# Attention and two feed-forward layers: the products with w_in by seven block products instead of eight

## The chip, the cores and the metric

The kernel runs on one core of one Trainium2 chip. The metric is the device time of one execution in microseconds (us). TensorE (PE) multiplies matrices, its weight loads are listed as PEld; VectorE (DVE), ScalarE (ACT) and GpSimd (POOL) work on elements; SyncE (SP) issues the DMAs. A "column" is one column of the moving operand of a matmul, 128 deep.

## The reference

```python
scores = scale * np.matmul(q, k.transpose(0, 1, 3, 2))          # 4 batches, 8 heads, 576 tokens, 64 wide
cum = np.cumsum(np.log(np.clip(f, 0.0001, 1.0)), axis=-1)
scores = np.where(causal, -1000000000.0, scores + cum[:, :, :, None] - cum[:, :, None, :])
attn = softmax(scores)                                           # row maximum taken off, sum + 1e-9
x = (attn @ v).transpose(0, 2, 1, 3).reshape(2304, 512)
h = x @ moe_w_in;  x = (h - np.tanh(h)) @ moe_w_out              # w_in 512 x 2048, w_out 2048 x 512
h = x @ moe2_w_in; return (h * (1 / (1 + np.exp(-h)))) @ moe2_w_out
```

The weights arrive in double precision, the other inputs in single.

## The kernel before

**Attention** takes about the first 179 us. It goes over 16 pairs of heads, nine tiles each (144 tiles, then a tail), and puts its result, features on partitions, into `x` of 4 x 2304 columns. The list `ahead` places work of the feed-forward part between its tiles, counted from the last tile: weight loads and decoding, the split of the first inputs, and the first twelve pieces of products with w_in (`hidden`).

**High and low parts.** A single-precision operand is kept as two tiles of the type TensorE multiplies: the high part is a cast on ScalarE, the low part the rest, a subtraction on VectorE. A product is three matmuls, high x high, high x low and low x high, into one sum in PSUM. The doubles are decoded into such pairs by seven steps on ScalarE and VectorE (`wstages`).

**Feed-forward.** The 2048 hidden features are 16 chunks of 128, in three sets a layer (`SETS`); the tokens are five groups (four of 512, one of 256). Loops: layer, set, group, chunk. A step multiplies the group's four input tiles with the chunk's w_in (`hidden`, 12 matmuls into one PSUM bank), two steps later its gate with the chunk's w_out (`project`, 12 matmuls into accumulators of PSUM). Between, `gate` computes h - tanh(h) in layer 0 (tanh on ScalarE, line 268, the difference on VectorE, line 269) or silu in layer 1 (line 271), the cast of the high part (line 272) and the low part (line 275). At a set's end the accumulators are copied or added to the total, a tile `y` for layer 0; layer 1's goes back into `x`, and its last set through `ob` (three buffers, line 320) to the output, one DMA of 256 KB for each 128 tokens. Inputs are split once for each set and group (`xsplit`).

**Order.** It is written out by hand: every engine executes its instructions in the order of the program. `front(n)` issues step n's w_in products, the next group's split, step n - 1's gate, and a share of the decoding for the next set; `project` follows.

Of the kernel before, what the change touches and what calls it, by code (L numbers as in the profile page):

```python
# [39 lines left out]
def forgetting_attention_two_ffn(  # L40
# [81 lines left out]
    z = x.rearrange("p k t -> p (k t)").rearrange("p (m d) -> p m d", d=DM)  # L122
    ys = []

    wtiles, raws = {}, {}  # L130

    chunks = [(l, c) for l in range(2) for c in range(NFC)]

    def wload(k, ms=(0, 1)):
        if k >= len(chunks):
            return
        l, c = chunks[k]
        for m in ms:
            r = rawp.tile([P, DM, 2], U32, tag="raw", name=f"raw{l}_{c}_{m}")
            nc.sync.dma_start(out=r.rearrange("p n w -> p (n w)"), in_=(w_in, w_out)[m][l][c])  # L140
            raws[k, m] = r

    def wstages(k):

        l, c = chunks[k]
        slot = k % NSLOT
        tag = {m: f"{l}_{c}_{m}" for m in range(2)}
        a, b, w = {}, {}, {}

        def scale(m):  # L150
            high = rd(raws[k, m][:, :, 1])
            nc.scalar.activation(high, high, AF.Prelu, scale=2.0 ** -112, alpha=-(2.0 ** 32))

        def shift(m):
            a[m] = wtmp.tile([P, DM], U32, tag="wa", name=f"wa{tag[m]}")
            nc.vector.tensor_scalar(a[m], raws[k, m][:, :, 1], 3, None, ALU.logical_shift_left)

        def split(m):
            hi, lo = w[m] = [
                wpool[slot].tile([P, DM], F32R, tag=f"w{s}{slot}_{m}", name=f"w{s}{tag[m]}") for s in "hl"  # L160
            ]
            nc.scalar.copy(hi, rd(a[m]))

        def exponent(m):
            b[m] = wtmp.tile([P, DM], F32, tag="wb", name=f"wb{tag[m]}")
            nc.vector.tensor_scalar(b[m].bitcast(U32), a[m], 0xFF800000, None, ALU.bitwise_and)

        def low(m):
            nc.vector.scalar_tensor_tensor(
                b[m], raws.pop((k, m))[:, :, 0], 2.0 ** -52, b[m], ALU.mult, ALU.mult  # L170
            )

        def rest(m):
            hi, lo = w[m]
            nc.vector.tensor_tensor(lo, rd(a[m]), rd(hi), ALU.subtract)

        def join(m):
            hi, lo = w[m]
            nc.vector.tensor_tensor(lo, rd(lo), b[m], ALU.add)
            wtiles[l, c, m] = (hi, lo)  # L180

        return [(fn, m) for fn in (scale, shift, exponent, low, split, rest, join) for m in range(2)]
# [560 lines left out]
```

## Time and profile before

| | |
|---|---|
| median of 3 runs | 968.22 us (968.2 to 968.56) |
| the profiled execution | 968.29 us |
| its span, first to last instruction | 966.5 us |
| busy TensorE / VectorE / ScalarE / POOL | 958.9 / 564.0 / 456.7 / 161.0 us |
| granted TensorE clock, mean | 0.999 |
| DMA | 56.67 MB, of it 64 weight tiles of 512 KB |

An engine's busy time is the union of its instructions. Matmuls overlap in the records, so the mean length of one is longer than the step from one start to the next. Idle time is put down to the engine whose work ended it.

### The profile page before, as it was taken

What the parts mean: (1) busy time and instruction counts of PE and PEld (TensorE: products, weight loads), DVE (VectorE), ACT (ScalarE), POOL (GpSimd) and SP (SyncE); (2) the same over time, 40 slices, a digit from 0 to 9 for tenths busy, and PEclk for the clock granted to TensorE, in tenths of its full rate; (3) what the DMA queues carried; (4) which work ended last, traced back from release to release, by engine and by line L of the source; (5) the groups of instructions that cost most, each with busy time, mean ns of one, the idle gap of its engine ahead of it and who ended that gap; (6) DMA issues with size and microseconds to landing.
All of it is one profiled execution on the core that took longest, in us unless ns stands there. A gap on an engine that the chain in (4) does not pass through costs nothing.

```text
span 966.5 us, 13852 instructions
## 1 busy us (share of the span) xinstructions
PE 958.9 (99%) x5208; PEld 791.4 (82%) x5208; DVE 564.0 (58%) x1243; ACT 456.7 (47%) x979; POOL 161.0 (17%) x244
## 2 busy tenths in 40 slices
PE   8999999999999999999999999999999999999998
PEld 6777777789888889888888888888888888888887
DVE  7788888767764657555767743344344555523323
ACT  6788888545444334333434443344344443433322
POOL 8999999100000000000000000000000000000000
PEclk9999999999999999999999999999999999999999
DMA  5343342221210111110122101010111110001111
GB/s 165 140 137 125 125 161 81 107 87 45 88 44 1 44 45 44 44 44 0 44 87 82 50 1 44 22 66 0 44 44 44 44 44 1 1 1 43 44 44 66
DMA packets 21698, 56.67 MB, mean 59 GB/s; under 512 B 6848, under 2 KB 6848, under 8 KB 21600
## 3 DMA queue, kind: packets, MB, share of 16 engines
q1 hardware_dynamic: 21624, 55.77, 16.8%
q8 instruction: 41, 0.67, 0.3%
q14 instruction: 25, 0.20, 0.1%
q10 hardware_dynamic: 8, 0.02, 0.0%
HBM read 49.35 MB, written 5.31 MB: 57 GB/s over the span
## 4 chain that ended last, share of the span: by engine, by line
PE 98%; DVE 1%; POOL 0%; DMA 0%; issue 0%; ACT 0%; POOLq 0%
PE h L254 41%; PE a L312 41%; PE t L494 5%; PE s L447 5%; PE out_t L550 4%; PE s L439 2%; PE out L550 0%; PE out_t L578 0%; DMA de<-x 0%; DVE x L113 0%; DVE x L111 0%; DVE p L460 0%; DVE de L571 0%; DVE x L117 0%; POOL p L482 0%
## 5 line engine op out<-in xcount | busy, mean ns | idle before, releaser
L254 PE MATMUL h<-xh,wh 128*128 128x512 f32 (+1 forms) x640 | 236.0, 369 | 0.0
L254 PE MATMUL h<-xl,wh 128*128 128x512 f32 (+1 forms) x640 | 235.6, 368 | 0.0
L254 PE MATMUL h<-xh,wl 128*128 128x512 f32 (+1 forms) x640 | 235.4, 368 | 0.0
L275 DVE TENSOR_TENSOR gl<-g,gh 128x512 fp32r<-128x512 f32 (+1 forms) x160 | 101.9, 637 | 103.4 <-ACT gh L272 101.6
L254 PEld LDWEIGHTS h<-xh,wh 128*128 128x128 f32 x640 | 120.7, 189 | 20.7
L254 PEld LDWEIGHTS h<-xl,wh 128*128 128x128 f32 x640 | 120.6, 188 | 20.4
L254 PEld LDWEIGHTS h<-xh,wl 128*128 128x128 f32 x640 | 120.6, 188 | 20.1
L272 ACT CAST gh<-g 128x512 fp32r<-128x512 f32 (+1 forms) x160 | 92.6, 579 | 92.8 <-DVE g L269 90.2
L312 PE MATMUL a<-gl,wh 128*128 128x512 f32 (+1 forms) x320 | 117.8, 368 | 0.0
L312 PE MATMUL a<-gh,wh 128*128 128x512 f32 (+1 forms) x320 | 117.7, 368 | 0.0
L312 PE MATMUL a<-gh,wl 128*128 128x512 f32 (+1 forms) x320 | 117.7, 368 | 0.0
L312 PE MATMUL a<-wh,gh 128*128 128x512 f32 x288 | 112.2, 390 | 0.0
L312 PE MATMUL a<-wl,gh 128*128 128x512 f32 x288 | 112.2, 390 | 0.0
L312 PE MATMUL a<-wh,gl 128*128 128x512 f32 x288 | 112.0, 389 | 0.0
L271 ACT ACTIVATE g<-h 128x512 f32<-128x512 f32 (+1 forms) x80 | 44.3, 554 | 115.3 <-PE h L254 95.2
L242 DVE TENSOR_TENSOR xl<-y,xh 128x512 fp32r<-128x512 f32 (+1 forms) x60 | 37.4, 638 | 96.4 <-ACT xh L240 96.4
L240 ACT CAST xh<-y 128x512 fp32r<-128x512 f32 (+1 forms) x60 | 34.2, 580 | 105.4 <-PE h L254 103.7
L468 ACT ACTIVATE p<-p,mn 128x128 f32<-128x128 f32 (+3 forms) x128 | 71.2, 558 | 15.1 <-DVE mn L460 12.7
L482 POOL TENSOR_SCALAR p<-p,sm 128x128 f32<-128x128 f32 (+3 forms) x128 | 71.4, 577 | 8.6 <-DVE sm L479 7.9
L242 DVE TENSOR_TENSOR xl<-x,xh 128x512 fp32r<-128x512 f32 (+1 forms) x56 | 34.5, 634 | 63.9 <-ACT xh L240 63.9
L460 DVE CUSTOM_DVE_ANT_0 p<-s,mask 128x128 f32<-128x128 f32 (+3 forms) x128 | 59.5, 480 | 20.1 <-PE s L447 20.1
L312 PEld LDWEIGHTS a<-gh,wh 128*128 128x128 f32 x320 | 60.3, 189 | 10.1
(89 smaller groups left out, 1368.7 us busy)
## 6 DMA issues: line engine op xcount, KB each, us to landing
raw<-w_in SPq DMA_DIRECT2D x32, 512.0 KB
raw<-w_out SPq DMA_DIRECT2D x32, 512.0 KB
kqraw<-kq SPq DMA_DIRECT2D x16, 608.0 KB
vraw<-v SPq DMA_DIRECT2D x16, 320.0 KB
out<-ob SPq DMA_DIRECT2D x18, 256.0 KB
lq<-kqs SPq DMA_DIRECT2D x32, 32.0 KB
dec<-x SPq DMA_DIRECT2D x1, 576.0 KB
de<-dec SPq DMA_DIRECT2D x28, 17.0 KB
```

Of the source, the lines that this page charges most:

```text
L242: eng.tensor_tensor(lo[:, :n], src[:, k, t0:t0 + n], rd(hi[:, :n]), ALU.subtract)
L254: nc.tensor.matmul(hp[:, :n], w[:, k * P:k * P + P], m[:, :n], start=(k == 0 and r == 0), stop=(k == NKT - 1 and r == 2),)
L271: nc.scalar.activation(g[:, :n], hp[:, :n], AF.Silu)
L272: nc.scalar.copy(gh[:, :n], g[:, :n])
L275: nc.vector.tensor_tensor(gl[:, :n], g[:, :n], rd(gh[:, :n]), ALU.subtract)
L312: nc.tensor.matmul(dst, w, m, start=(first and r == 0), stop=(last and r == 2))
L447: nc.tensor.matmul(s[:, h, c:c + n], a[half(h), q], b[half(h), 0:n], start=r == 0, stop=r == 3,)
L460: nc.vector.tensor_tensor_reduce(out=pt.rearrange("p (g c) -> p g c", g=2) if i == 4 else pt, in0=src, in1=m, op0=ALU.add, op1=ALU.min, sc ...
L468: nc.scalar.activation(pt, pt, AF.Exp, bias=mn, scale=-1.0, accum_out=sums[:, n // 3 % 5, n % 3, 0:1],)
L482: nc.gpsimd.tensor_scalar(pt, pt, sm[:, j:j + 1], 1.0, ALU.mult, ALU.mult)
L494: nc.tensor.transpose(t[:, k], pt[:, c * P:c * P + P], ident)
L550: nc.tensor.matmul(dst, vraw[p][:, h, D * c:D * c + D], ptfs[p % 2][:, h, 448 * c + a:448 * c + q1], start=c == 0, stop=c == last,)
```

## The change

The products with w_in are done in Strassen's way (with Winograd's sums). A block is 768 tokens; its input is a 2 x 2 of blocks (two halves of the 512 features, 256 each, by two halves of the tokens, 384 each), and the weights of two chunks are a 2 x 2 too (two chunks by two halves of the features). Seven products replace eight. Their operands are sums and differences of blocks: four sums of weights on VectorE for each pair of chunks, four differences of inputs for each block of tokens (`xtemp`), and the products are combined by seven additions on VectorE (`add`), which also take them off PSUM; product 1 is copied by ScalarE.

Loops: layer, set (now four sets of two pairs), block (three), pair. One pair for one block is a **slot**, 48 in all; a layer, set and block is a unit of two slots. A slot is fifteen pieces, seven products (six matmuls of 384 columns each) and eight pieces G of products with w_out ("halves") that belong to gates of the slots before: `P1 G P6 G P2 G G P7 G P5 G P4 G P3 G`. In layer 0 a half is six matmuls of 384 columns; in layer 1 six or three of 512. Slot 0 has no halves, slot 1 has two; after the last slot 14 halves follow.

The seven operands of a block, each split into high and low, are made in the first set of a layer (`xmake`), and written to DRAM, 786 KB each; in the other sets each is loaded again (`xload`) after its last product of the unit before. Every operand has one buffer. The weights' decoding works on two chunks at once, with low and high joined before the sums, and is spread over the pieces by a table (`fills`). The attention tail has no products with w_in any more; it makes the first block's operands and decodes pair 1. Accumulators have two buffers of two banks, products four of one bank. The first set's totals are copied by ScalarE, all others are added by VectorE. There is no `y`: layer 0's result goes into `x` again. `ob` has one buffer, for two output tiles.

```diff
-HL = 2
-NEARLY, MID, LATE = 2, 3, 6
-SETS = ((5, 6, 5), (6, 5, 5))
+NB, TB, TH = 3, 768, 384
+KA = {1: 1, 2: 2, 3: 6, 4: 0, 5: 3, 6: 4, 7: 5}
...
-    rawp = ctx.enter_context(tc.tile_pool(name="rawp", bufs=4))
-    wtmp = ctx.enter_context(tc.tile_pool(name="wtmp", bufs=3))
+    rawp = ctx.enter_context(tc.tile_pool(name="rawp", bufs=2))
+    wtmp = ctx.enter_context(tc.tile_pool(name="wtmp", bufs=1))
...
+            to, p, op, r = ((4, 0, ALU.add, 1), (6, 2, ALU.subtract, 0),
+                            (5, 4, ALU.subtract, 2), (7, 3, ALU.subtract, 5))[part]
+            nc.vector.tensor_tensor(s[:, to], s[:, p], s[:, r], op)
...
+    for s in range(2 * NSET):
+        e, o, k = 2 * s + 2, 2 * s + 3, 6 * s
+        first = s == 0
+        plan = {
+            1 + first: jobs(e, 0, [("scale",)], PRE),
+            2 + first: jobs(e, 0, SUMS, HILO) + jobs(e, 1, [("scale",)]),
+            3 + first: jobs(e, 1, PRE, LAST),
+            4 + first: jobs(o, 0, [("scale",)], PRE, SUMS),
+            6: jobs(o, 1, PRE),
+        }
+        plan[5] = plan.get(5, []) + jobs(o, 0, HILO) + jobs(o, 1, [("scale",)])
+        for d, js in plan.items():
+            fills.setdefault(k + d, []).extend(js)
+        late.add(k + 7)
+        fills.setdefault(k + 7, []).extend(jobs(o, 1, LAST))
+    fills[0] = jobs(1, 0, HILO) + jobs(1, 1, [("scale",)], PRE)
+    fills[1] = jobs(1, 1, LAST)
...
+        to, p, m = ((t1, b12, b11), (t2, b22, t1), (t1, b22, b12), (t2, b21, t2))[k - 1]
+        nc.vector.tensor_tensor(to, p, m, ALU.subtract)
...
+        nc.scalar.copy(t[:, 0], frm)
+        (eng or nc.vector).tensor_tensor(t[:, 1], frm, rd(t[:, 0]), ALU.subtract)
+        d = xd[l, b, i] = dram.tile([P, 4 * TH], F32, name=f"xd{l}_{b}_{i}")
+        nc.sync.dma_start(out=d, in_=rd(t).rearrange("p r k t -> p (r k t)"))
+
+    def xload(u, i):
+        l, s, b = units[u]
+        t = xtile(u, i)
+        nc.sync.dma_start(out=rd(t).rearrange("p r k t -> p (r k t)"), in_=xd[l, b, i])
...
+        if s == 0:
+            xat(2 * u - 2, 5, xtemp, l, b, 1)
+            xat(2 * u - 2, 6, xtemp, l, b, 2)
+            for p, i in ((2, 1), (4, 6), (6, 2)):
+                xat(2 * u - 1, p, xmake, u, i)
+            xat(2 * u - 1, 7, xtemp, l, b, 4)
+            xat(2 * u - 1, 11, xmake, u, 5)
+            xat(2 * u - 1, 12, xtemp, l, b, 3)
+            xat(2 * u - 1, 13, xmake, u, 7)
+            xat(2 * u, 0, xmake, u, 4)
+            xat(2 * u, 2, xmake, u, 3)
+        else:
+            for i, p in PIECE.items():
+                xat(2 * u - 1, p, xload, u, i)
...
+        if s == 0:
+            nc.scalar.copy(total, acc)
+        elif l == 0 or s + 1 < NSET:
+            nc.vector.tensor_tensor(total, acc, total, ALU.add)
+        else:
+            ob = wtmp.tile([P, 2, DM], F32, tag="wb", name=f"ob{u}_{h}_{g}")
...
+    def bend(u, j, h):
+        l = units[u][0]
+        t = pools["tp"].tile([P, 2, TH], F32, tag=f"t{h}", name=f"t{u}_{j}_{h}")
+        nc.scalar.activation(t, hs[h], AF.Silu if l else AF.Tanh)
         if l == 0:
+            nc.vector.tensor_tensor(t, hs[h], t, ALU.subtract)
...
+                i = int(what[1])
+                dst = product(u, j, i)
+                if i == 1:
+                    nc.scalar.copy(half_tile(u, j, 0)[:, 1], dst)
+                    rest()
+                elif i == 6:
+                    add(half_tile(u, j, 1)[:, 0], dst, hs[0][:, 1])
+                elif i == 2:
+                    add(hs[0][:, 1], dst, hs[0][:, 1])
+                elif i == 7:
+                    add(hs[0][:, 0], dst, hs[1][:, 0])
+                elif i == 5:
+                    add(hs[1][:, 1], dst, hs[1][:, 0])
+                    add(hs[1][:, 0], dst, hs[0][:, 0])
+                elif i == 4:
+                    add(hs[0][:, 0], dst, hs[0][:, 0])
+                    bend(u, j, 0)
+                else:
+                    add(hs[1][:, 1], dst, hs[1][:, 1])
+                    high(u, j, 0)
+                    low(u, j, 0)
+                    bend(u, j, 1)
+                    left.extend([(high, (u, j, 1)), (low, (u, j, 1))])
+            for fn, a in xplan.get((sl, p), []):
+                fn(*a)
+            for job in todo[slice(*share.get(p, (0, 0)))]:
+                fill(job)
...
-            for i in range(3):
-                for k in range(NKT):
-                    at(4 * i + k, hidden, i, [k])
...
+            for n, i in ((-11, 1), (-8, 2)):
+                at(n, xmake, 0, i, nc.gpsimd)
+            for n, k in ((-1, 1), (0, 2), (2, 4), (4, 3)):
+                at(n, xtemp, 0, 0, k)
+            for n, i in ((1, 6), (3, 5), (5, 7), (6, 4), (7, 3)):
+                at(n, xmake, 0, i)
+            for k, job in enumerate(jobs(1, 0, [("scale",)], PRE, SUMS)):
+                at(8 + k, fill, job)
```

The fills go in equal shares behind ten pieces of a slot (1 to 7, 11, 12 and 14, counted from 0). `PRE` is shift, exponent, low and join; `HILO` the high and low parts of the seven w_in operands in two portions each; `LAST` those of w_out.

## Rows read from the trace of the kernel before

**Rows 1.** Page, busy us and share; then forty slices, tenths; GB/s a slice.

```profile
PE 958.9 (99%) x5208; PEld 791.4 (82%) x5208; DVE 564.0 (58%) x1243; ACT 456.7 (47%) x979; POOL 161.0 (17%) x244
...
PE   8999999999999999999999999999999999999998
...
PEclk9999999999999999999999999999999999999999
...
GB/s 165 140 137 125 125 161 81 107 87 45 88 44 1 44 45 44 44 44 0 44 87 82 50 1 44 22 66 0 44 44 44 44 44 1 1 1 43 44 44 66
```

**Rows 2.** Page, chain that ended last, shares of the span by line.

```profile
PE h L254 41%; PE a L312 41%; PE t L494 5%; PE s L447 5%; PE out_t L550 4%; PE s L439 2%; PE out L550 0%; PE out_t L578 0%; DMA de<-x 0%; DVE x L113 0%; DVE x L111 0%; DVE p L460 0%; DVE de L571 0%; DVE x L117 0%; POOL p L482 0%
```

**Rows 3.** Timeline of TensorE around 223 us: start us, us, engine, operation.

```profile
221.00 0.39 PE L312 MATMUL a<-gh,wh 128*128 128x512 f32 x1
...
223.72 0.28 PE L254 MATMUL h<-xh,wh 128*128 128x256 f32 x1
...
225.15 0.40 PE L312 MATMUL a<-gh,wh 128*128 128x512 f32 x1
```

**Rows 4.** Groups by form, TensorE: count | busy us, mean ns | idle us.

```profile
L254 PE MATMUL h<-xh,wh 128*128 128x512 f32 x512 | 199.9, 390 | 0.0
...
L312 PE MATMUL a<-wh,gh 128*128 128x512 f32 x288 | 112.2, 390 | 0.0
...
L312 PE MATMUL a<-gh,wh 128*128 128x512 f32 x256 | 99.7, 389 | 0.0
...
L254 PE MATMUL h<-xh,wl 128*128 128x256 f32 x128 | 36.2, 283 | 0.0
...
L312 PE MATMUL a<-gh,wh 128*128 128x256 f32 x64 | 18.1, 282 | 0.0
```

**Rows 5.** Timeline of VectorE, 184 to 190 us; in brackets idle us and releaser.

```profile
184.52 1.28 DVE L169 SCALAR_TENSOR_TENSOR wb<-raw,wb 128x512 f32<-128x512 uint32 x2
185.72 1.29 DVE L175 TENSOR_TENSOR wl<-wa,wh 128x512 fp32r<-128x512 f32 x2
...
189.50 0.69 DVE L275 TENSOR_TENSOR gl<-g,gh 128x512 fp32r<-128x512 f32 x1 [0.69 <-ACT gh L272]
```

**Rows 6.** Groups by form, VectorE and ScalarE.

```profile
L275 DVE TENSOR_TENSOR gl<-g,gh 128x512 fp32r<-128x512 f32 x128 | 88.4, 690 | 91.5 <-ACT gh L272 89.9
L272 ACT CAST gh<-g 128x512 fp32r<-128x512 f32 x128 | 79.6, 622 | 74.9 <-DVE g L269 72.8
...
L166 DVE TENSOR_SCALAR wb<-wa 128x512 uint32<-128x512 uint32 x64 | 26.6, 442 | 0.0
...
L275 DVE TENSOR_TENSOR gl<-g,gh 128x256 fp32r<-128x256 f32 x32 | 13.5, 421 | 11.8 <-ACT gh L272 11.7
L272 ACT CAST gh<-g 128x256 fp32r<-128x256 f32 x32 | 13.0, 407 | 17.9 <-DVE g L269 17.4
```

**Rows 7.** Timelines of POOL, TensorE and VectorE, end of attention.

```profile
171.21 0.75 POOL L482 TENSOR_SCALAR pt<-pt,sm 128x576 f32<-128x576 f32 x1
...
171.33 0.48 PE L254 MATMUL h<-xh,wh 128*128 128x512 f32 x1
...
176.16 0.40 PE L254 MATMUL h<-xh,wl 128*128 128x512 f32 x1
...
176.65 2.76 PE L550 MATMUL out_t<-ptf,vraw 128*64 128x512 f32 x20
...
177.41 0.28 DVE L539 COPY ptf<-t 128x128 f32<-128x128 f32 x1
```

**Rows 8.** Timeline of VectorE, last output adds.

```profile
949.54 2.06 DVE L321 TENSOR_TENSOR ob<-a,x 128x512 f32<-128x512 f32 x3 [3.36 <-PE a L312]
952.41 0.69 DVE L321 TENSOR_TENSOR ob<-a,x 128x512 f32<-128x512 f32 x1 [0.81 <-DMA out<-ob]
```

**Rows 9.** Chain of waits in order of time, its last piece: start us, us.

```profile
962.77 0.69 DVE ob L321
```

**Rows 10.** DMA rate, 300 to 400 us, in 40 slices of 2.5 us.

```profile
GB/s 7 0 0 0 0 0 0 0 0 0 0 285 141 0 0 0 0 3 3 67 143 0 0 182 34 0 0 0 33 338 56 0 0 0 0 0 28 270 121 0
```

More of the change, by code (lines that the diff above doesn't have):

```diff
@@ L121, in forgetting_attention_two_ffn @@
     x = xpool.tile([P, NKT, NT], F32, name="x")
[L122 to L182, printed above, removed]
@@ L219, in forgetting_attention_two_ffn @@
-    pools, xs, hps, gts, accs = {}, {}, {}, {}, {}
-    def ends(i):
-        si, c = steps[i][1], steps[i][5]
-        c0 = sum(SETS[steps[i][0]][:si])
-        return c == c0, c == c0 + SETS[steps[i][0]][si] - 1
+    units = [(l, s, b) for l in range(2) for s in range(NSET) for b in range(NB)]
+    NSL = 2 * len(units)
+    pools = {}
     def open_pools(bank=None, **bufs):
@@ new lines, in forgetting_attention_two_ffn, with wload, wdo @@
+    raws, wtiles, wjobs = {}, {}, {}
+    ODD_FIRST = (1, 0)
+    def wload(q, m, parts=(0, 1)):
+        if q >= 2 * NPR:
+            return
+        l, c = divmod(2 * q, NFC)
+        if (q, m) not in raws:
+            raws[q, m] = rawp.tile([P, 2, DM, 2], U32, tag="raw", name=f"raw{q}_{m}")
+        for i in parts:
+            to = raws[q, m][:, i].rearrange("p n w -> p (n w)")
+            nc.sync.dma_start(out=to, in_=(w_in, w_out)[m][l][c + ODD_FIRST[i]])
+    def wdo(q, *names):
+        for name in names:
+            wjob(q, *name)
@@ new lines, in forgetting_attention_two_ffn, with jobs @@
+    PRE = [(w,) for w in ("shift", "exponent", "low", "join")]
+    SUMS = [("sum", k) for k in range(4)]
+    HILO = [("hi", 0), ("hi", 1), ("lo", 0), ("lo", 1)]
+    LAST = [("hi",), ("lo",)]
+    def jobs(q, m, *lists):
+        return [(q, m) + j for js in lists for j in js] if q < 2 * NPR else []
+    fills, late = {}, set()
+    for s in range(2 * NSET):
[13 more added lines that the diff above has]
+        fills.setdefault(k + 7, []).extend(jobs(o, 1, LAST))
@@ new lines, in product @@
+    def product(u, j, i):
+        q = 2 * (u // NB) + j
+        wih, wil = (w[:, KA[i]] for w in wtiles[q, 0])
+        xh, xl = xo[u, i][:, 0], xo[u, i][:, 1]
+        dst = pools["ps_h"].tile([P, 512], F32, tag="h", name=f"h{u}_{j}_{i}")[:, 0:TH]
+        for k in range(2):
+            ks = slice(k * P, k * P + P)
+            for r, (w, m) in enumerate(((wih, xh), (wih, xl), (wil, xh))):
+                nc.tensor.matmul(dst, w[:, ks], m[:, k], start=k == 0 and r == 0, stop=k == 1 and r == 2)
+        return dst
```

300 lines of the change are left out of this document (169 added, 131 removed).

## The prediction

> **What bounds the kernel now.** I read the busy line and the slices first. TensorE's queue is never empty: 99% busy, nine tenths in every slice but the first and last, at a granted clock of nine tenths or more, while VectorE has 58% and ScalarE 47% over the span [rows 1]. A busy TensorE need not be a limiting one, so the chain of waits comes next: its TensorE lines add up to 98%, 41% of it the products with w_in (line 254) and 41% those with w_out (line 312) [rows 2]. Third, the step between starts, because a matmul's listed length (390 ns at 512 columns) overlaps its neighbours. Twelve matmuls of 512 columns take 223.72 - 221.00 = 2.72 us, 226.7 ns each; twelve of 256 take 225.15 - 223.72 = 1.43 us, 119.2 ns each [rows 3]. Both are the columns at 2.4 GHz (213.3 and 106.7 ns) plus some 13 ns. The weight load of each matmul is hidden, or the shorter ones could not step at 119 ns. So 384 columns, half-way between, get 173.0 ns.
>
> **1. TensorE's work.** Before, the feed-forward part holds, by its groups: with w_in 3 x 512 at 512 columns and 3 x 128 at 256; with w_out, layer 0, 3 x 256 at 512 and 3 x 64 at 256; layer 1, 3 x 288 at 512 [rows 4]. That is 3168 x 0.2267 + 576 x 0.1192 = 718.2 + 68.7 = 786.9 us. After: 48 slots (24 units of three blocks, four sets and two layers, two pairs of chunks each) of 7 products x 6 matmuls = 2016 at 384 columns; layer 0's w_out 12 units x 96 = 1152 at 384; layer 1's 864 at 512, as before. 3168 x 0.1730 + 864 x 0.2267 = 548.1 + 195.9 = 744.0 us. **Term: -42.9 us**, if TensorE stays the bound. An eighth of the w_in columns goes (46 us at 2.4 GHz), and 288 more matmuls of 13 ns give 4 back.
>
> The Trainium skill, "TensorE: Matmul & The Clock Gate", section "Back-to-back issue gap", has an isolated gap of N/2.4 + 2.5 ns; by it the sum would be 746.6 - 701.3, a gain of 45.3 us. The trace's 226.7 ns at 512 is 11 above that figure, so the rows decide.
>
> **2. VectorE's work by slot.** Back to back, VectorE starts two 512-column tensor operations every 1.20 us (184.52 and 185.72), 0.60 each, less than the listed 0.69 because ends overlap [rows 5, 6]. At 256 columns 0.42 - 0.09 = 0.33. The line through both gives 0.47 at 384, 0.87 at 768, 1.13 at 1024. Single-source integer operations are listed at 442 ns for 512 [rows 6], less the same 0.09 some 0.34, and double to 0.60 at 1024.
> - Per slot: seven adds of 384 (3.3), two low parts of 768 (1.7), in layer 0 two subtractions after tanh (1.7): 6.7 in layer 0, 5.0 in layer 1.
> - Weights of one pair: w_in 0.6 + 0.6 + 1.13 + 1.13, four sums at 0.33, low parts 0.87 + 1.13, in all 6.8; w_out 0.6 + 0.6 + 3 x 1.13 = 4.6. 11.4 over three slots: 3.8 a slot, at most 4.8 as the list of fills lays it.
> - Adding the accumulators to the total (sets 1 to 3): 3.5 a unit, 1.7 a slot.
> - First set only: four differences and seven low parts of 768 per block: 9.5 a unit, 4.8 a slot.
> - Waits on ScalarE: the subtraction stands right behind its tanh. At 512 columns a wait of 0.69 for a cast of 0.62 is seen now [rows 5]; ScalarE's 0.62 and 0.41 at 512 and 256 [rows 6] make 0.51 at 384 and 0.84 at 768, so this wait is 0.95 a slot in layer 0. The other low part (its high part is cast after the next slot's first product) is covered by a fill or costs up to 0.9.
>
> So sets 1 to 3 of layer 0 take 6.7 + 3.8 + 1.7 + about 1.2 = 13.5 us a slot (worst 14.5), layer 1 some 11.5. A slot of TensorE is 90 x 0.173 = 15.6 us (42 x 0.173 + 36 x 0.2267 = 15.4 in layer 1). TensorE stays the bound there, with one to two us of slack, and four PSUM buffers let it run about seven us ahead of a late add. ScalarE has four operations of 768 and one of 384 (3.9 us), 1.6 of weights and at most 4 of operands or totals a slot, under 10. I take 2 us for scattered waits over all these slots, bounds 0 and 18 (a full us in each of layer 0's).
>
> **3. The start.** In slots 0 and 1 there is almost nothing with w_out to multiply: TensorE has 42 x 0.173 = 7.3 and 54 x 0.173 = 9.3 us. VectorE has the next blocks' operands and pair 1's weights on top: slot 0: 6.7, fills 5.5, two differences 1.7, wait 1.0, less a low part that slips (0.9) = 14.2; slot 1: 6.7, five low parts 4.3, two differences 1.7, a fill 1.1, waits 1.2 = 15.1. Where VectorE starts: now POOL's last normalisation ends at 171.96 and attention's last copy off PSUM at 177.7; between 171.33 and 176.16 TensorE starts twelve of the early w_in matmuls (2.8 us) [rows 7]. Without those I put the copy at 174.8; then two low parts (1.7) and a fill list (4.8) stand ahead of slot 0: 181.4. Followed add by add, with TensorE four products ahead at most, slot 1 of VectorE ends at 210.7 and TensorE begins slot 2 at 201.2. There it waits 1.5 us for half 4 (its gate comes out at 207.8) and the seventh operand, and at the same place in slot 4 2.8 us, because slot 3 gives VectorE 17.2 us (sums, low parts, the third block's operands). Slot 6 begins at 266.9. Without a loss: TensorE's attention ends now at 176.65 + 2.76 = 179.41, and the feed-forward matmuls from there to the end take 962.77 - 179.41 = 783.4 of 786.9 [rows 7, 9], so 3.5 lay ahead and the clean start is 175.9; slots 0 to 5 are 78.9, hence 254.8. **Term: +12.1 us**, bounds 5 (VectorE starts 3 us earlier and its waits are covered) and 20 (attention's end doesn't move up and each ACT wait counts).
>
> The moved matmuls no longer fill gaps of the attention's last transposes. If the chain over POOL, copies and values doesn't close up by those 3.5 us, TensorE loses what is missing: 0 to 3.5, I take **+0.5**.
>
> **4. Layer 1's first set.** Slots 22 to 27 carry operands again: VectorE has 16.1, 17.7, 14, 17.7 us in slots 22 to 25 against 15.6. The accumulators' sum in slot 24 comes 2.9 us late for the next accumulation in the same banks. **+3**, bounds 0 and 8.
>
> **5. Operands from DRAM.** Sets 1 to 3 read 7 x 786 KB = 5.5 MB a unit, each operand right after its last product and one slot ahead of its next. Requests are 2.2 us apart. The busiest 2.5 us now moved 338 GB/s [rows 10], 2.3 us for 786 KB; with a slot's lead even 195 GB/s is in time (seven at 4 us each end 29 us after the first, when the seventh product starts). Cost nothing; gone is the cover only under that rate. SyncE's queue waits for a product before each load; a weight load behind it is late by at most a product, with three slots to spare.
>
> **6. The end.** `ob` has one buffer for three, and an output of two tiles. Now the fourth output add waits for the first DMA: 949.54 + 0.69 to 952.41 is 2.2 us for 256 KB; 512 KB takes 2.9 with 0.8 more at 338 GB/s [rows 8, 10]. After the last slot 14 halves remain with no product between them. The first of the last eight waits 0.6 us for an add of 1024 columns, the second 2.2 for the other add, which waits for the DMA: 2.8. Then from the last matmul: add 1.2 less 0.7 overlap, DMA 2.9, add 0.7, and 3.0 to the span's end as now (962.77 + 0.69 to 966.5): 7.1 instead of 966.5 - 962.77 = 3.7 [rows 9]. **Together +6.2**, bounds 2 and 9.
>
> **Sum.** -42.9 + 2 + 12.1 + 0.5 + 3 + 6.2 = -19.1 us. The profiled execution took 968.29 (span 966.5 and 1.8 around it), 0.07 from the median of 968.22, so both give **949.2 us**.
>
> **Rivals.**
> - *VectorE becomes layer 0's bound* (the other side). Place: tanh to subtraction, high to low part, with listed lengths for steps (dependent operations don't overlap): adds 7 x 0.56, 768s 4 x 0.96, weights 4.3, sum 1.9 make 14.0; waits 1.0 + 1.0 and an ACT queue that is late by 1 give 17. It decides from 15.6 + 19.1/24 = 16.4 us a slot. For it: now 91.5 us of VectorE's idle time stand before its 512-column low parts, 89.9 of it put down to ScalarE [rows 6]. Against: ScalarE's own slot is short, and now both engines follow a TensorE that sets the pace. Price: 24 x 1.4 + 6 in the first sets' slots: about 989. A milder one, 0.5 us a slot: 961.
> - *VectorE never matters*: start 5, end 2, the rest nothing: -42.9 + 5 + 2 = -35.9, 932; with half of what the forecast loses beyond that, 941. For: the idle time above. Against: slots 0 and 1 hold 29 us of VectorE for 17 of TensorE.
> - *The clock falls in slots 0 and 1.* It is at full level now in all slices, and TensorE nowhere waits [rows 1]; after, it is busy about half of 25 us there. At 1.2 GHz its 16.6 us double to 33, 4 over VectorE's 29: 954. The Trainium skill, same page, section "Why this matters for your kernels", warns of idle gaps between bursts; no run here shows one.
> - *Operands come late.* At the 165 GB/s of the busiest slice on the page [rows 1], seven loads last 33 us against 31 a unit: 18 x 2.5 = 45 us: 994. Against: 338 GB/s seen.
>
> **How the numbers follow.** Forecast 0.57 (own range 940 to 958), mild VectorE 0.09, VectorE never 0.12, clock 0.08, VectorE bound 0.10, DRAM 0.04. Range 936 to 966 leaves out the two slow cases and a little below. 0.2% is about 2 us, what a measurement can tell from no change. Faster 0.84, same 0.03, slower 0.13.
>
> **What would show it.** TensorE's matmuls at 384 columns start every 173 ns; idle TensorE of some 15 us, almost all in slots 0 to 5, released by VectorE's adds and low parts; VectorE near 100% there and 80 to 90% in layer 0's later slots; busy VectorE about 730 us for 564; span end 7 us after the last matmul; over 130 MB more DMA. Wrong, if TensorE waits in slots 8 to 20, if 384 columns step above 180 ns, or if waits for DMA appear on operands.

## The result, and the profile after

The changed kernel takes **976.02 us** (median of five runs, 972.9 to 980.34) where the kernel before, run beside it, takes 968.22 (968.18 to 968.56): ratio 1.0082, 95% interval 1.0054 to 1.0111. It is **slower by 0.8%**, where 949.2 was predicted, and above the range. The profiled run is the quickest of the five: 972.9 us, span 971.1, clock 0.989; against its own span the prediction (947.4) is 23.7 us short.

The page of the changed kernel answers [rows 1, 2]: busy time with its share, three rows of forty slices, memory traffic, and the two rows of the chain that ended last (shares by engine and by line).

```profile
PE 935.5 (96%) x5496; PEld 848.0 (87%) x5496; DVE 740.0 (76%) x1338; ACT 436.4 (45%) x782; POOL 160.5 (17%) x242
...
PE   8999999779999999999999989899999999999996
...
DVE  7788887899888887888788988785676677765442
...
PEclk9999999899999999999999999999999999999998
...
HBM read 148.44 MB, written 38.34 MB: 192 GB/s over the span
...
PE 82%; DVE 10%; ACT 3%; issue 2%; POOL 1%; DMA 1%; POOLq 0%; DVEq 0%; ACTq 0%
PE a L314 35%; PE h L346 30%; PE t L594 5%; PE s L547 4%; PE out_t L650 4%; DVE hs L379 3%; PE s L539 2%; PE out_t L678 1%; DVE xt L242 1%; DVE xo L256 1%; ACT t L356 1%; DMA out<-ob 1%; DVE wl L194 1%; DVE t L358 1%; DVE ob L334 1%
```

TensorE lost only 23.4 us of busy time (958.9 before), not 42.9, and stands idle for 35.6 us of the span, 7.6 before. VectorE is busy 740.0 us (730 predicted) and has 10% of the chain: the products are still the bound, but there are places where VectorE is. Transfers went from 57 to 189 MB; no wait for an operand's load appears in the list of waits.

The groups that answer to [rows 4, 6] (count | busy, mean ns of one | idle before it and its releaser):

```profile
L346 PE MATMUL h<-xo,wh 128*128 128x384 f32 x1344 | 345.9, 338 | 8.0 <-DVE hs L379 8.0
...
L379 DVE TENSOR_TENSOR hs<-h,hs 128x384 f32<-128x384 f32 x336 | 185.3, 553 | 84.7 <-PE h L346 80.3
...
L314 PE MATMUL a<-wh,gh 128*128 128x512 f32 x288 | 112.8, 392 | 6.4 <-ACT x L328 3.5
```

Two stretches of TensorE's timeline answer to [rows 3], one of layer 0 and one of layer 1 (start us, us, operation; a row with x2 joins two matmuls):

```profile
410.86 0.51 PE L346 MATMUL h<-xo,wh 128*128 128x384 f32 x2
...
412.94 0.51 PE L346 MATMUL h<-xo,wh 128*128 128x384 f32 x2
...
702.53 0.39 PE L314 MATMUL a<-wh,gh 128*128 128x512 f32 x1
...
703.92 0.51 PE L346 MATMUL h<-xo,wh 128*128 128x384 f32 x2
...
704.97 0.39 PE L314 MATMUL a<-wh,gh 128*128 128x512 f32 x1
```

In layer 0 twelve matmuls take 2.08 us: 173 ns each, as predicted. In layer 1 the six of 512 columns take 703.92 - 702.53 = 1.39 us (232 ns, not 226.7) and the six of 384 take 1.05 (175).

Then I cut the span at the first matmul of each slot. The stretches below are slots 0, 1, 2, then 6 of layer 0, then 24 and 26, where layer 1 begins (stretch, length, busy time and count of PE, PEld, DVE, ACT, POOL, then granted clock, DMA share, GB/s).

```profile
180.31:193.09 12.78, 9.32 (x47) 8.71 (x43) 10.74 (x16) 4.96 (x6) 0.00 (x0) 0.87 0.53 200
193.09:209.73 16.64, 12.07 (x55) 10.89 (x55) 15.37 (x22) 6.87 (x9) 0.00 (x0) 0.90 0.45 169
209.73:229.90 20.17, 17.54 (x91) 17.13 (x91) 17.28 (x24) 10.51 (x14) 0.00 (x0) 0.92 0.46 187
276.70:292.30 15.60, 15.60 (x91) 15.60 (x91) 12.48 (x19) 9.09 (x12) 0.00 (x0) 1.00 0.60 249
559.09:578.51 19.42, 15.95 (x92) 15.58 (x91) 18.17 (x24) 7.64 (x11) 0.00 (x0) 1.00 0.40 163
594.45:615.50 21.05, 17.60 (x80) 15.31 (x79) 18.15 (x27) 10.41 (x14) 0.00 (x0) 0.92 0.51 200
```

Slots 3 to 21 all last 15.60 us, with TensorE busy throughout and VectorE on average 84% (73 to 92%). Beside a late end of attention and slightly longer steps in layer 1, the loss is in three places: slots 0 to 2, slots 22 to 26, and the end. In slot 1 VectorE is busy 15.4 of 16.6 us, in slot 24 18.2 of 19.4: there TensorE waits for it. Where the clock column is below 1.00, part of a slot ran at half clock: TensorE's busy time is 17.54 us in slot 2 and 17.60 in slot 26, where slots without a wait have 15.60 and 15.73. A wait at full clock adds 0.35 as well (slot 24, 15.95), so about 1.6 and 1.5 us are the clock's. What ended TensorE's waits (engine, line, what it waited for: us in total, times, longest):

```profile
PE h L346 <- DVE hs L379: 8.0, 5, 2.5
...
PE a L314 <- DVE x L330: 4.5, 3, 3.5
...
PE a L314 <- DVE wl L194: 2.6, 1, 2.6
```

The sum of the prediction beside the profiled run, in us of span:

| step | predicted | measured | from |
|---|---|---|---|
| TensorE's work | -42.9 | -36.4 | slots 6 to 21 +0.03 each; 27 to 47 15.73 for 15.44, +0.29 each |
| scattered waits | +2 | 0 | slots 3 to 21 without one |
| end of attention | +0.5 | +4.4 | slot 0 starts at 180.31, clean 175.9 |
| start, slots 0 to 5 | +12.1 | +17.5 | slot 6 at 276.70 for 254.8, less 4.4 |
| layer 1's first set | +3 | +11.4 | slots 22 to 26 89.2 for 77.8 |
| end | +6.2 | +7.4 | slot 45 and, with the last halves, 47: +0.6, +3.4; after the last matmul 7.1 for 3.7 |
| sum | -19.1 | +4.3 | spans 971.1 - 966.5 = +4.6; 0.3 is not placed |

### The profile page after: what moved, and what is told of

Same layout as the page of the kernel before. It is cut to its first block, busy times and chain, and to the rows that moved or that the text cites. A ratio compares the mean times of both kernels' runs of the same rounds, so it can differ in the third digit from the quotient of the medians.

```text
span 971.1 us, 14858 instructions
## 1 busy us (share of the span) xinstructions
PE 935.5 (96%) x5496; PEld 848.0 (87%) x5496; DVE 740.0 (76%) x1338; ACT 436.4 (45%) x782; POOL 160.5 (17%) x242
## 4 chain that ended last, share of the span: by engine, by line
PE 82%; DVE 10%; ACT 3%; issue 2%; POOL 1%; DMA 1%; POOLq 0%; DVEq 0%; ACTq 0%
PE a L314 35%; PE h L346 30%; PE t L594 5%; PE s L547 4%; PE out_t L650 4%; DVE hs L379 3%; PE s L539 2%; PE out_t L678 1%; DVE xt L242 1%; DVE xo L256 1%; ACT t L356 1%; DMA out<-ob 1%; DVE wl L194 1%; DVE t L358 1%; DVE ob L334 1%
## 5 line engine op out<-in xcount | busy, mean ns | idle before, releaser
L346 PE MATMUL h<-xo,wh 128*128 128x384 f32 x1344 | 345.9, 338 | 8.0 <-DVE hs L379 8.0
L346 PEld LDWEIGHTS h<-xo,wh 128*128 128x128 f32 x1344 | 247.8, 190 | 24.2 <-DVE hs L379 7.5
L379 DVE TENSOR_TENSOR hs<-h,hs 128x384 f32<-128x384 f32 x336 | 185.3, 553 | 84.7 <-PE h L346 80.3
L356 ACT ACTIVATE t<-hs 128x768 f32<-128x768 f32 x96 | 81.3, 847 | 355.3 <-DVE hs L379 355.3
L346 PE MATMUL h<-xo,wl 128*128 128x384 f32 x672 | 226.8, 337 | 0.0
L314 PE MATMUL a<-gh,wh 128*128 128x384 f32 x384 | 129.4, 337 | 4.5 <-DVE x L330 4.5
L314 PE MATMUL a<-gh,wl 128*128 128x384 f32 x384 | 129.4, 337 | 2.6 <-DVE wl L194 2.6
L314 PE MATMUL a<-gl,wh 128*128 128x384 f32 x384 | 129.3, 337 | 0.0
L346 PEld LDWEIGHTS h<-xo,wl 128*128 128x128 f32 x672 | 127.3, 189 | 0.0
L369 DVE TENSOR_TENSOR gl<-t,gh 128x768 fp32r<-128x768 f32 x96 | 91.5, 953 | 41.9 <-ACT gh L365 41.7
```

The source lines that it names most:

```text
L314: nc.tensor.matmul(dst, w, m, start=first and r == 0, stop=last and r == 2)
L346: nc.tensor.matmul(dst, w[:, ks], m[:, k], start=k == 0 and r == 0, stop=k == 1 and r == 2)
L356: nc.scalar.activation(t, hs[h], AF.Silu if l else AF.Tanh)
L369: nc.vector.tensor_tensor(gl, hs[h], rd(gh), ALU.subtract)
L379: nc.vector.tensor_tensor(to, p, s, ALU.add)
```

## Where VectorE's delay begins

The end of attention, which answers to [rows 7], on POOL, VectorE and ScalarE (in brackets the idle time before and its releaser):

```profile
171.52 2.66 POOL L582 TENSOR_SCALAR p<-p,sm 128x512 f32<-128x512 f32 x2 [1.91 <-PE out_t L650]
174.16 1.44 POOL L582 TENSOR_SCALAR pt<-pt,sm 128x576 f32<-128x576 f32 x1
...
170.09 0.96 DVE L256 TENSOR_TENSOR xo<-xt,xo 128x768 fp32r<-128x768 f32 x1 [0.94 <-ACT xo L255]
...
171.15 0.17 DVE L579 RECIPROCAL sm<-sm 128x3 f32<-128x3 f32 x1
171.25 0.93 DVE L242 TENSOR_TENSOR xt<-x,xt 128x768 f32<-128x768 f32 x1
...
177.27 0.28 DVE L639 COPY ptf<-t 128x128 f32<-128x128 f32 x1
...
182.08 0.69 DVE L161 TENSOR_SCALAR wa<-raw 128x1024 uint32<-128x1024 uint32 x1 [2.05 <-ACT raw L157]
...
187.53 1.21 DVE L379 TENSOR_TENSOR hs<-h,hs 128x384 f32<-128x384 f32 x2
...
180.43 0.59 ACT L658 COPY x<-out_t 128x512 f32<-128x512 f32 x1 [1.42 <-PE out_t L650]
180.91 1.14 ACT L157 ACTIVATE raw<-raw 128x1024 f32<-128x1024 f32 x1
```

ScalarE's same copy in the kernel before:

```profile
179.46 0.59 ACT L558 COPY x<-out_t 128x512 f32<-128x512 f32 x1 [2.38 <-PE out_t L550]
```

POOL's last normalisation ends at 174.16 + 1.44 = 175.6, 3.6 us later than before, for two reasons. It begins late: it needs the reciprocals of row sums, line 579 of VectorE, and the last of them (171.15) stands in VectorE's queue behind a low part that itself waits 0.94 us for ScalarE (170.09). (The row of 171.52 names TensorE's line 650 as releaser; its last matmul ends at 171.35 and the reciprocal at 171.32, so the rows can't tell which of the two held POOL.) And it runs slowly, 1.44 us for the 0.75 of before [rows 7], while VectorE makes differences of inputs (171.25 and on). VectorE's last copy off PSUM (line 639), the one from which the prediction counts, ends at 177.55, hardly earlier than the 177.69 of before, where 174.8 was predicted. Two low parts follow, the first after 0.65 us of waiting for ScalarE. ScalarE's copy of attention's last result (line 658) comes at 180.43, 1.0 us later than before, and behind it stands the first step of pair 1's decoding (180.91); VectorE is idle 2.05 us for it and then decodes for 5.5 us. Its first add of slot 0 comes at **187.53; the prediction had 181.4**.

## The experiments

All ratios are to the kernel before, 968.2 us, run beside each.

**1. Is it the clock in slots 0 and 1?** Spare matmuls fill the places where slots 0 and 1 have no half; their result is used by nothing.

```diff
+        for k in range(4):
+            nc.tensor.matmul(spare[sl][:, 0, 0:TH], wih[:, 0:P], xo[u, i][:, 0, 0], start=True, stop=True)
...
                 if n0 + g >= 0:
                     project(n0 + g)
+                else:
+                    idle(sl, u, j, pieces[p - 1] if pieces[p - 1] != "G" else pieces[p - 2])
```

> Four spare matmuls of 384 columns (their sums are never read) in each of the 14 places of slots 0 and 1 that have no half. If the fallen clock is a loss of its own: no step of about 320 ns is left in slots 0 to 2, where 39 of them cost 5.2 us now, and slot 3 starts 4 to 6 us earlier (224 to 226 for 229.9); the median goes down by 4 to 7 us to 969 to 972, with less spread than 972.9 to 980.3. If the clock costs nothing because VectorE sets the pace there anyway: slot 3 starts at 229 to 231 and the time stays within 1.5 us.

979.67 us (median of four; 975.78 to 980.38), ratio 1.011 (1.009 to 1.013). The stretches of its slots 0 and 1:

```profile
179.70:192.66 12.96, 12.96 (x79) 12.96 (x76) 10.90 (x16) 4.94 (x6) 0.00 (x0) 1.00 0.55 207
192.66:207.56 14.90, 14.08 (x80) 13.44 (x80) 13.76 (x20) 6.89 (x9) 0.00 (x0) 1.00 0.36 145
```

The clock is full in slots 0 and 1 (0.87 and 0.90 without the spare matmuls), yet slot 3 begins at 229.18 instead of 229.90. In these two slots the clock is worth at most 0.7 us; VectorE sets the pace. Slot 2, which has all its halves, still waits 2.6 us for a low part and shows 0.92. The median is 3.7 us above the changed kernel's, more than the 1.5 expected; in the profiled run the loss arises from slot 24 on, in places that the edit leaves as they were.

**2. Does attention's end hang on the order in VectorE's queue?** Differences and the first low part are issued earlier, pair 1's first decoding step stands ahead of the last copies.

```diff
-            for n, k in ((-1, 1), (0, 2), (2, 4), (4, 3)):
+            for n, k in ((-9, 1), (-7, 2), (-3, 4), (3, 3)):
                 at(n, xtemp, 0, 0, k)
-            for n, i in ((1, 6), (3, 5), (5, 7), (6, 4), (7, 3)):
+            for n, i in ((-5, 6), (1, 5), (5, 7), (6, 4), (7, 3)):
                 at(n, xmake, 0, i)
+            at(2, fill, (1, 0, "scale"))
...
```

> In attention's tail, three differences and one operand of the first block move ahead of the last tiles, and the scaling of pair 1's weights ahead of attention's last copies. If VectorE's queue delayed the softmax sums there and ScalarE's queue the weights: attention ends on TensorE at 177 to 178 (180.3 now, 179.4 before the change), VectorE's first addition starts at 182 to 183 (187.5), and the time falls by 4 to 6 us. If the missing early products are the reason, or POOL's own operand work: attention's end stays at 180 and the time within 2 us.

974.6 us (973.59 to 977.11), ratio 1.007 (1.0053 to 1.0087). Slot 0 begins at 178.81, slot 3 at 227.59, 1.5 and 2.3 us earlier than in the profiled run of the changed kernel. The seven kernels below and above whose attention is the same as the changed one's (experiments 1, 3 to 7) begin slot 0 between 179.70 and 182.46, so this start lies outside their spread, 0.9 to 3.7 us ahead of theirs (experiment 8's kernel, with the same order, has 178.85). VectorE's first add comes at 183.97 (expected: 182 to 183), 3.6 us earlier, for pair 1's decoding no longer waits for ScalarE, and slot 2 begins 3.6 us earlier too. Slot 2 itself, at clock 0.84, then gives 1.3 back. The 1.4 us off the median are inside the spread of the changed kernel's runs, and the 4 to 6 expected did not come. POOL's last two rows of this kernel:

```profile
171.57 2.06 POOL L582 TENSOR_SCALAR p<-p,sm 128x512 f32<-128x512 f32 x2 [1.74 <-ACT x L658]
173.61 0.75 POOL L582 TENSOR_SCALAR pt<-pt,sm 128x576 f32<-128x576 f32 x1
```

They start where they did (171.57 for 171.52), because the low part ahead of the last reciprocal still waits for ScalarE, but take 2.06 and 0.75 us for 2.66 and 1.44, 1.3 us less: the changed kernel has two differences and a low part of VectorE beside them, this one a single difference. Half right: what the edit took away is the slowing of POOL. POOL's late start remains, and its cause is read from the order of the rows, not removed in a run.

**3. Can POOL take the operands?** In all units but the first, POOL makes the differences and low parts.

```diff
-        nc.vector.tensor_tensor(to, p, m, ALU.subtract)
+        (eng or nc.vector).tensor_tensor(to, p, m, ALU.subtract)
...
+            xat(2 * u - 2, 5, xtemp, l, b, 1, nc.gpsimd)
...
+                xat(2 * u - 1, p, xmake, u, i, nc.gpsimd)
```

> Differences and low parts of the input operands of all blocks but the first go from VectorE to POOL, which is idle then. If VectorE is what holds up the start and the beginning of layer 1: slots 0 to 2 (49.6 us, 32.2 clean) lose some 7 us, slots 22 to 26 (89.2 us, 77.8 clean) some 9, together 14 to 17: 958 to 962. If POOL (1.83 us for a low part, 20 us a unit) or a port that it shares with VectorE takes its place: less than 4 us gained, with TensorE waiting for operands.

976.82 us (975.71 to 978.9), ratio 1.0091 (1.0076 to 1.0106): no gain. VectorE's groups by form between 220 and 290 us, first of the changed kernel, then of this one, and POOL's group in this one:

```profile
L379 DVE TENSOR_TENSOR hs<-h,hs 128x384 f32<-128x384 f32 x34 | 18.6, 551 | 2.2 <-PE h L346 1.8
...
L181 DVE TENSOR_TENSOR ws<-ws 128x256 f32<-128x256 f32 x8 | 3.1, 418 | 0.1
```

```profile
L379 DVE TENSOR_TENSOR hs<-h,hs 128x384 f32<-128x384 f32 x30 | 16.3, 551 | 0.6
L181 DVE TENSOR_TENSOR ws<-ws 128x256 f32<-128x256 f32 x8 | 8.6, 1107 | 0.1
...
L256 POOL TENSOR_TENSOR xo<-x,xo 128x768 fp32r<-128x768 f32 x4 | 8.7, 2164 | 6.0 <-ACT xo L255 6.0
```

Sums of weights grow from 418 to 1107 ns, the low parts of weights of 768 columns from 952 to 1770, while the adds of products, one of whose inputs lies in PSUM, stay at 551. Slots 0 to 2 took 45.4 us for 49.6, but slots 3, 24 and 26 took 21.3, 17.4 and 23.5: what VectorE no longer does comes back as longer operations and late sums. The Trainium skill, "SBUF — State Buffer", section "Who interferes with whom", says that a VectorE operation with two inputs in SBUF contends with a GpSimd one that reads SBUF and that one with at most one SBUF input, outside VectorE's two-port modes, does not. This trace agrees for the adds (551) and for the sums and low parts (1107 and 1770). The integer operations of line 165, which have one SBUF input, grew too, from 685 to 1364 ns; whether they ran in such a mode no run here shows.

**4. Is it VectorE's operand work at all?** In all units but the first the differences are left out, and ScalarE copies the low parts instead; operands that were differences are taken from blocks of x.

```diff
+        if (l, b) != (0, 0):
+            return
...
+        if u:
+            nc.scalar.copy(t[:, 1], frm)
+        else:
             (eng or nc.vector).tensor_tensor(t[:, 1], frm, rd(t[:, 0]), ALU.subtract)
```

> For all blocks but the first of layer 0, the four differences are left out and the low parts are copies by ScalarE, so the output is not the reference's; products, spills and loads stay. If VectorE's operand work (9.5 us a unit) is what holds up the beginnings of the layers, without a POOL in the way: slots 22 to 26 take 78 to 80 us (89.2 now, 77.8 clean), slot 3 starts at 221 to 225 (229.9), the time falls by 14 to 18 us to 956 to 961. If the beginnings are held up by the weights' decoding or by ScalarE's queue: less than 5 us.

957.23 us (956.31 to 958.15), ratio 0.9886 (0.9867 to 0.9906). Its slots 2 and 24:

```profile
208.59:224.19 15.60, 15.60 (x91) 15.60 (x91) 9.89 (x15) 10.89 (x16) 0.00 (x0) 1.00 0.54 217
551.79:567.39 15.60, 15.60 (x92) 15.60 (x91) 11.74 (x17) 10.40 (x15) 0.00 (x0) 1.00 0.52 206
```

Slots 22 to 26 take 78.1 us with no wait (89.2 before the edit, 77.8 clean), and slot 2 takes 15.60 (20.17). So the loss there is VectorE's work, not the loads or the clock. 957 is not the price of a real kernel: slots 0 and 1 still take 27.7 us (29.4) and the end its waits.

**5. The copy in slot 26.** Here two in-order queues meet. ScalarE and TensorE of the changed kernel:

```profile
608.68 1.04 ACT L192 CAST wh<-ws 128x1024 fp32r<-128x1024 f32 x1 [4.59 <-DVE ws L181]
609.64 1.49 ACT L328 COPY x<-a 128x1024 f32<-128x1024 f32 x2
...
610.70 0.50 PE L314 MATMUL a<-wh,gh 128*128 128x512 f32 x1 [3.45 <-ACT x L328]
```

ScalarE's copy of the first totals of layer 1 (line 328) stands behind the cast of weights (line 192), which waits 4.59 us for VectorE's sums (line 181); TensorE needs the copy's banks and waits 3.45. The edit gives layer 1's first set the delayed decoding plan that layer 0's already has.

```diff
-        first = s == 0
+        first = s % NSET == 0
```

> The decoding for layer 1's second set begins one slot later (26 and not 25). If VectorE's overload in slot 25 (17.7 us by my count) and its lateness after it cause the waits of slots 24 to 26: these take 49 to 52 us (56.4 now) and the time falls by 4 to 7 us. If the wait belongs to ScalarE's queue, where the copy of layer 1's first totals stands behind a cast that waits for the weights' sums, it moves with the sums to slot 27 and less than 2 us is gained.

971.42 us (969 to 972.82), ratio 1.003 (1.0017 to 1.0043). Slots 24 to 26 take 19.41 + 15.61 + 15.86 = 50.9 us for 56.4: slot 26 is clean, slot 24 stays. The first theory holds for slots 25 and 26, but slot 24's wait is not among what it explains.

**6. The output buffer.** VectorE's last two output adds and the last matmul of the changed kernel, which answer to [rows 8, 9], stand below the edit:

```diff
-            ob = wtmp.tile([P, 2, DM], F32, tag="wb", name=f"ob{u}_{h}_{g}")
+            ob = wtmp.tile([P, 2, DM], F32, tag=("wb", "wa")[g], name=f"ob{u}_{h}_{g}")
```

```profile
963.36 1.23 DVE L334 TENSOR_TENSOR ob<-a,x 128x1024 f32<-128x1024 f32 x1 [6.51 <-PE a L314]
...
963.61 0.39 PE L314 MATMUL a<-wh,gl 128*128 128x512 f32 x1
...
967.52 0.69 DVE L334 TENSOR_TENSOR ob<-a,x 128x512 f32<-128x512 f32 x1 [2.94 <-DMA out<-ob]
```

> The two output tiles of a half block lie in different buffers, so that the second addition does not wait for the DMA of the first. Theory: the wait of 2.2 us among the last 14 halves goes, the end after the last matmul shrinks from 7.1 to about 4 us, and the waits of 0.5 to 2.6 us that stand in slots 44 to 46 of some runs go too: 5 to 7 us less. Rival (the DMA itself sets the end): less than 2 us.

969.98 us (median of ten; 967.67 to 972.14), ratio 1.0016 (1.0006 to 1.0026). The same stretch now:

```profile
962.68 1.82 DVE L334 TENSOR_TENSOR ob<-a,x 128x1024 f32<-128x1024 f32 x2 [7.29 <-PE a L314]
...
962.93 0.39 PE L314 MATMUL a<-wh,gl 128*128 128x512 f32 x1
```

The second add no longer waits 2.94 us; from the last matmul's end to the span's end 4.9 us remain of 7.1, slot 47 takes 31.14 for 33.37 (to the last matmul's end), slot 45 15.73 for 16.33: 5.0 us together. The first theory holds.

**7. Where do layer 1's 0.29 us a slot come from?** First, fewer changes between products and halves: layer 1's pieces go in pairs.

```diff
-                pieces = "P1 G P6 G P2 G G P7 G P5 G P4 G P3 G".split()
+                pieces = ("P1 G G P6 P2 G G P7 P5 G G P4 P3 G G" if u >= len(units) // 2 else ...).split()
```

> In layer 1 the eight halves stand in pairs: TensorE changes between 384 and 512 columns four times a slot and not seven. If each change costs about 0.04 us: a layer 1 slot takes 15.61 us (15.73 now; 15.44 by steps of 173.3 and 226.7 ns), 2 to 3 us in all. If the longer steps belong to the operands' place in memory or to traffic: 15.73 stays.

975.12 and 975.28 us in two runs, ratio 1.0072 (1.0052 to 1.0092); slots of 15.68 to 15.71 us for 15.73. Not a price per change. Second, layer 1's halves multiply only 384 of their 512 columns, except in the first matmul of each sum:

```diff
+                n = TH if l and not (first and r == 0) else m.shape[-1]
-                nc.tensor.matmul(dst, w, m, start=first and r == 0, stop=last and r == 2)
+                nc.tensor.matmul(dst[:, 0:n], w, m[:, 0:n], start=first and r == 0, stop=last and r == 2)
```

> Layer 1's halves use 384 of the 512 columns in all but the first matmul of each sum, so a quarter of the output lacks most of its terms. In layer 1 a slot takes 15.73 us where steps of 173.3 and 226.7 ns make 15.44. If the excess comes of mixing 384 and 512 columns: the 384-column steps in layer 1 are 173 to 174 ns, as in layer 0, except beside the few that are still 512 wide. If it comes of how the operands lie (gate tiles as weights, w_out as moving operand): they stay at 175 to 179 ns, products included.

941.59 us in one run, with a kernel that leaves out terms. Undisturbed slots take 13.72 us; three of a slot's 78 matmuls keep 512 columns, so steps at full pace make 75 x 0.1730 + 3 x 0.2267 = 13.66: the excess falls from 0.29 to 0.06. The tiles and the places of the operands are the same, so the excess belongs to 512 columns beside 384. The changed kernel's own end says the same: behind slot 47's last product, 28 steps of 512 columns with no product between them take 952.24 - 945.89 = 6.35 us, 226.8 ns each. By what mechanism stays open.

**8. The mends of 2, 5 and 6 together**, with pair 1's last low part (for which slot 2 waits 2.6 us) issued at pieces 1 and 3 of slot 1.

```diff
+        if sl == 1:
+            hooks = [1, 3]
         share = {p: (
```

> The later decoding, the two output buffers, the tail's order of the earlier experiment, and pair 1's last weight step at the beginning of slot 1 (half 4 waits 2.9 us for it). If the four losses are separate: 974 to 976 less 5, 6, 1.5 and 2, that is 959 to 963, under the kernel before. If one loss covers another (VectorE's lateness shows up at the next place): 966 to 970.

961.07 us (960.65 to 962.09), ratio 0.9928 (0.9913 to 0.9942): now **faster than before**. By medians the mends add up: alone they took 1.4, 4.6 and 6.0 us off, together with the earlier low part 15.0. But the trace doesn't show the low part as the fourth of them. Slot 2 takes 17.51 us for 20.17, with no step at half clock, but slots 3, 4 and 6 now take 17.13, 16.24 and 16.13 for 15.60, 2.7 us in all, and slot 7 begins 3.5 us earlier than in the changed kernel, by as much as VectorE's first add (184.01 for 187.53). In slot 3 TensorE waits 1.2 us for ScalarE's copy of totals, in slots 4 and 6 for low parts of VectorE. There one loss did cover another: up to slot 6 these two engines set the pace.

**9. Pair 1 decoded during attention.** Its loads and steps move to the pairs of heads before, four steps a pair of heads for three.

```diff
-            for k, job in enumerate(todo):
-                at(NTILE * (4 + k // 3) + (1, 3, 5)[k % 3] - N, wjob, *job)
+            todo += jobs(1, 0, [("scale",)], PRE, SUMS) + jobs(1, 1, [("scale",)], PRE)
+            for k, job in enumerate(todo):
+                at(NTILE * (4 + k // 4) + (1, 3, 5, 7)[k % 4] - N, ...)
...
-    fills[0] = jobs(1, 0, HILO) + jobs(1, 1, [("scale",)], PRE)
+    fills[0] = jobs(1, 0, HILO) + jobs(1, 1, LAST)
```

> The version with later decoding, two output buffers and the reordered tail, and now pair 1's weights are decoded during attention as far as their buffers allow (four decoding steps a pair of heads for three), so slots 0 and 1 have 8.3 us less of VectorE. If VectorE alone sets the pace there: slots 0 to 2 take 37 to 39 us (44.9 in the version before, 32.2 clean), and the time is 953 to 956. If attention, where VectorE is 85% busy, pays for it: attention ends 3 us or more later and less than 3 us are gained (959 to 962).

958.36 us (958.14 to 958.72), ratio 0.99 (0.9883 to 0.9916). Its slots 0 and 1:

```profile
182.85:190.27 7.42, 7.42 (x47) 7.42 (x43) 4.52 (x7) 2.75 (x4) 0.00 (x0) 1.00 0.60 242
190.27:205.77 15.50, 12.08 (x55) 10.82 (x55) 13.88 (x20) 6.77 (x9) 0.00 (x0) 0.89 0.28 114
```

Slots 0 to 2 take 38.7 us (44.9 in the run before), slot 0 with no wait, but attention ends 4.0 us later (182.85 for 178.85): the same work now stands ahead of row sums (a reading of the order, not tested apart). Both theories hold in part; 2.7 us are left of 6.2.

**10. Layer 0's last set decodes earlier**, so that slots 22 to 24 carry less.

```diff
+        if s == NSET - 1:
+            plan[1] += jobs(e, 0, SUMS)
+            plan[2] = jobs(e, 0, HILO) + jobs(e, 1, [("scale",)], PRE)
+            plan[3] = jobs(e, 1, LAST) + plan.pop(4)
```

> On top of that, the decoding in layer 0's last set is drawn forward so that slot 22 has none. If VectorE's surplus over slots 22 to 24 (16.1, 17.7, 14 us for 15.6) makes the late totals: slots 22 to 24 take 47 to 49 us (53.8 before, 46.8 clean) and the time falls by a further 4 to 6 us. If slots 19 to 21, now at about 15.6 us of VectorE, wait instead: less than 2 us.

**957.06 us** (955.73 to 957.15), ratio 0.9882 (0.9867 to 0.9897): the quickest kernel that computes the whole function, 1.2% under the kernel before. Slots 22 and 23 are clean, but slot 21 now takes 17.21 and slot 24 19.68: 68.1 us for slots 21 to 24 instead of 69.4. The work is moved, not hidden.

## Why the prediction was wrong

- **The step that failed is "where VectorE starts": 187.53 for 181.4.** The prediction took the early w_in matmuls out of TensorE's queue, let VectorE's last copy off PSUM move up with them to 174.8, and put two low parts and a list of decoding behind it without a wait. First, the copy did not move up: it ends at 177.55, 2.75 us late. Differences and a low part now stand between attention's own steps on VectorE, which executes in order, and POOL's last normalisation ends 3.6 us later than before instead of earlier; the bound "0 to 3.5" was on TensorE's gaps and not on VectorE's queue. Second, behind the copy VectorE waits 0.65 and 2.05 us for ScalarE, waits that the sum doesn't have. It took 177.7 for attention's last copy off PSUM, but that row of [rows 7] is VectorE's; ScalarE's comes at 179.46 there, and the first decoding step stands behind it. The work itself, 7.3 for 6.6, was nearly right.
- **What the runs show of this step.** Experiment 2 takes 3.6 of the 6.1 us away, and 1.5 of the 4.4 by which slot 0 starts late, of which 1.3 is the slowing of POOL; experiment 9 shows the inverse, more decoding ahead of the row sums and attention 4.0 us later. How much of the rest is the order of VectorE's queue is argued, not shown. VectorE's two slots were well sized: 14.9 and 15.7 us for 14.2 and 15.1. A late start passes through, because VectorE sets the pace there (experiment 1): in experiment 8 it starts 3.5 us earlier, and so does slot 7; in experiment 2, with more steps at half clock in slot 2, 2.3 of 3.6 us arrive.
- **Start, a second operand missed.** Slot 2's wait was priced at 1.5 us for half 4 and the seventh operand; it is 2.6 for the last low part of pair 1's w_out, which half 4 multiplies too. Steps at half clock behind it add about 1.6. Issuing the low part earlier gained nothing on balance (experiment 8). The 2.8 us of slot 4 never came, since TensorE was already late.
- **Layer 1's first set, mis-sized: +3 for 11.4.** Slot 24's wait was in it (2.9 for 3.5). Missed was what is queued behind a waiting instruction on ScalarE: the copy of slot 26, a wait of 3.45 us and about 1.5 of half clock behind it (with slot 25, experiment 5 takes 5.5 us off). Slots 22 and 23 lose 0.5 to 1 us each, for totals behind operands (experiment 4: none without them).
- **TensorE's work, mis-sized in layer 1.** The 173 ns were right, and slots 3 to 21 kept them for 296 us. That steps of 512 and 384 don't change by being mixed was assumed from [rows 3], where twelve of 512 stand beside twelve of 256; here it costs 0.29 us a slot, 6.1 in all (experiment 7).
- **The end** was predicted as it came: 7.1 us after the last matmul, exactly; the two waits before took 0.6 and 2.0. Missed was the same buffer in slot 45.
- **Scattered waits** of 2 us: none. **DRAM**: no wait, at up to 322 GB/s over a slot (slot 7).
- **Rivals.** In the changed kernel VectorE never holds TensorE up in slots 3 to 21, so it isn't layer 0's bound and that rival is out; it is the bound at the beginning of each layer (slots 0 to 2 and 22 to 26), which no case carried far enough. The clock rival was right about the clock, 0.87 to 0.92 in slots 0 to 2, and wrong about its price: at most 0.7 us in slots 0 and 1, and slot 2's 1.6 us come back as waits once they are gone (experiment 8). The half clock that did cost, about 1.5 us in slot 26, lies where it did not look.

## What to carry to other kernels

Work that is placed between the steps of a chain over several engines is priced by what stands behind it on its own queue, not by the engine's idle share: follow each result of the chain (here the row sums) past every instruction that is now ahead of it. A change that trades TensorE columns for VectorE work needs that sum for the stretches where the work piles up, and for the others a mean will do. When such a change disappoints, look for the few stretches that lost it: a changed order at three places and a second buffer turned +0.8% into -0.7%.
